# The output layer of the dense block by seven products a quad instead of eight, with sums held in PSUM banks and carried by ScalarE copies

## The chip, the cores and the metric

The kernel runs on one core of a Trainium2 chip (trn2). The metric is the device time of one execution in microseconds, from the median of several runs. The core has TensorE (PE in the profile, with PEld for its weight loads), VectorE (DVE), ScalarE (ACT), GpSimd (POOL) and SyncE (SP), whose queue issues nearly all DMAs.

## What is computed

```python
y = chunked_scan(x, a, B, C)                      # 4 x 8 heads, 768 tokens, 32 wide
x = y as 3072 tokens x 256
p = domain_probs / domain_probs.sum(-1)
out = sum over e < 4 of p[:, e] * (relu(x @ w1[e]) @ w2[e])       # w1: 256 x 1024, w2: 1024 x 256
g, val = out @ w_gate, out @ w_val                                # both 256 x 1536
result = (g / (1 + exp(-g)) * val) @ w_out                        # w_out: 1536 x 256
```

All of it is float32; the dense weights arrive as float64. The last two lines are the dense block. The change is in how its last product, with `w_out`, is formed.

## The kernel before

**Numbers.** A float32 operand is split into a high part (rounded by a ScalarE copy, `high`, or by the activation itself) and a low part (operand minus high part, `low`, one subtraction). A product of a 128x128 weight block with 512 tokens is three matmuls of 512 columns: high·high, low·high, high·low. "Product" below means such three matmuls; `product` (L932 to L936) issues them.

**Stages.** Until about 210 us the scan and the first expert units run. Then `blocks` of experts follow, 32 quads of 45 matmuls, until 552 us. Beside them `dense_quad` turns the float64 dense weights into split float32 blocks and sums of blocks, a step at a time, and stores them in DRAM (`wd_d`, `wo_d`); its steps stand in the table `todo` under slots, four to a quad. From 552.7 us the dense block runs: three pairs of token blocks (2 x 512 tokens each), and in each pair six quads of 256 hidden features, 18 quads.

**A dense quad.** The hidden layer of a quad is two halves, the gate and the value. Each is a 2x2 block product (two feature blocks by two token blocks, 256 inputs in two blocks) done with seven products in Winograd's form instead of eight (`seven`): A11·B11, S2·T2, S1·T1, S3·T3, A12·B21, S4·B22, A22·T4, where S and T are sums and differences of weight blocks and of token blocks made ahead. They go to four PSUM banks X, Y, Z, W (`h0`, `h1`, `h2`, `d0`), and VectorE adds the banks together through the SBUF tiles `c1`, `u` and `v`: `u` = Y + c1 (L957), `v` = Z + u (L959). The gate half adds `v` and `u` to W and Z (L1084) and takes Silu (L1085); the value half does the same adds (L1088) and multiplies with the gate's four results (L1090). Each of the four activations, named 11, 12, 21, 22 by feature block and token block, is split by `parts` (ScalarE L1095, GpSimd L1097).

**The output layer before.** `dense_project` (L1106 to L1131) multiplies each of the four split activations with two 128x128 blocks of `w_out` (two halves of the 256 outputs): eight products a quad, accumulated over the six quads of a pair in four banks (`d1`, `d2`, `o0`, `o1`). It lags a quad: `project_part` puts one activation, two products, at each of four places between the hidden products of the next quad. At the end of a pair the four banks are copied out and stored (`store`).

**What sets the order.** The program is recorded in order (`manual_schedule`) and each engine's queue is served in that order. A PSUM bank, an SBUF cell or a weight buffer is waited for by the instruction that needs it, and everything behind that instruction on its engine waits with it. Weights are loaded by SP two quads ahead (`dense_load`, 16 buffers in `wpool`). `dense_tokens` makes the split tokens and token sums of the next pair on ScalarE and GpSimd, spread over the quads by `dtodo`.

In the expert stage the seven products of a quad are already done with ScalarE copies that carry sums from bank to bank inside PSUM (`expert_hidden`):

```python
add(X, A11, "B11", True)
S.activation(out=Y, in_=X, func=AF.Copy)     # L996, then project_part: six matmuls
add(Y, S2, "T2")                             # accumulates on the copy
S.activation(out=Z, in_=Y, func=AF.Copy)     # L999
```

Of the kernel before, what the change touches and what calls it, by code (L numbers as in the profile page):

```python
# [7 lines left out]
F32 = mybir.dt.float32  # L8
# [16 lines left out]
def kernel(ctx: ExitStack, tc: tile.TileContext, nat_d, bc_d, bc0_d, a_d, probs, w1, w2, wg, wv, wo, out):  # L25
# [74 lines left out]
    wo_d = dram.tile([NQD, P, 2, 2 * DM], F32, name="wo_d")  # L100
# [503 lines left out]

    hid = {}
# [137 lines left out]
    def dense_quad(g, what):  # L743
# [34 lines left out]
        def s2():  # L778
            V.tensor_tensor(out=r["m"], in0=r["m"], in1=r["lo"], op=ALU.add)
            r["m"] = r["m"].bitcast(F32)  # L780
            if what < 2:
                r["s"] = r["f"].rearrange("p k n w -> p (k n w)").bitcast(F32)[:, :2 * FQ]
                gate_sums(r["m"], r["s"])

        def s3():
            if what < 2:
                r["out"] = [dpools["cv"].tile([P, W7], F32R, tag=f"w{z}", name=f"wd_{z}") for z in "hl"]
                high(r["out"][0][:, RAW], r["m"][:, P:])
            else:
                r["out"] = [dpools["cv"].tile([P, 2, 2 * DM], F32R, tag="wo", name="wd_o")]  # L790
                high(r["out"][0][:, 0, :], r["m"])

        def s4():
            if what < 2:
                low(r["out"][1][:, RAW], r["m"][:, P:], r["out"][0][:, RAW])
            else:
                low(r["out"][0][:, 1, :], r["m"], r["out"][0][:, 0, :])
# [7 lines left out]
        def store(z=None):  # L805
            if z is None:
                nc.sync.dma_start(out=wo_d[g], in_=r["out"][0].bitcast(F32))
            else:
                nc.sync.dma_start(out=wd_d[g, what, :, z, :], in_=r["out"][z].bitcast(F32))
# [6 lines left out]
    def dense_load(p, q):  # L816

        for what in range(3):
            if (p, q, what) in wq:
                continue  # L820
            if what < 2:
                hi, lo = (wpool.tile([P, W7], F32R, tag="w", name=f"wq_{z}") for z in "hl")
                for z, v in enumerate((hi, lo)):
                    nc.sync.dma_start(out=v.bitcast(F32), in_=wd_d[q, what, :, z, :])
            else:
                both = wpool.tile([P, 2, 2 * DM], F32R, tag="w", name="wq_o")
                nc.sync.dma_start(out=both.bitcast(F32), in_=wo_d[q])
                hi, lo = both[:, 0, :], both[:, 1, :]
            wq[p, q, what] = hi, lo


# [106 lines left out]
    def temp(tag):  # L938
        if tag == "c1":
            return mpool.tile([P, BN], F32, tag="mb", name=tag)  # L940
        return dpools["dt" if tag == "s" else "uv"].tile([P, BN], F32, tag=tag, name=tag, bufs=5 if tag == "s" else 1)

    pending = []

    def seven(p, w, out):

        X, Y, Z, W = (bank(*b) for b in (banks[0], banks[1], banks[2], banks[3]))
        V = nc.vector
        put = lambda ps, a, v, start: product(ps, w, a, operand(p, v), start)
        c1, u, v = temp("c1"), temp("u"), temp("v")  # L950
        put(X, A11, "B11", True)
        nc.scalar.activation(out=c1, in_=X, func=AF.Copy)
        for fn in pending:
            fn()
# [8 lines left out]
        def rest():  # L963
# [3 lines left out]
            if later[0]:  # L967
                later[0]()
# [435 lines left out]
```

## Time and profile before

| What | us |
|---|---|
| median of 3 runs (833.66 to 834.08) | 833.82 |
| span of the profiled execution, first to last instruction | 832.4 |
| a quad of experts without a wait, 45 matmuls | 10.20 |
| a dense quad, 66 matmuls | 14.96 |

For the profiled execution the page gives the span alone; the median of the timed runs is 1.42 us above it, and no other time of that execution is given. In the profile a matmul of 512 columns has a span of 0.39 us, but such matmuls are pipelined and start every 0.227 us, so spans must not be added up; distances between starts are what counts. ScalarE's spans overlap in the same way. DVE and POOL spans follow each other.

### The profile page before, as it was taken

How to read it: one execution, taken by the hardware profiler on the slowest of the kernel's cores; microseconds unless marked ns; L12 is line 12 of the kernel's file. 1: busy time of each engine (PE TensorE's matmuls, PEld its weight loads, DVE VectorE, ACT ScalarE, POOL GpSimd, SP SyncE). 2: the span in 40 equal slices, each digit the busy share in tenths (PEclk: the TensorE clock that was granted, in tenths of full speed). 3: DMA queues.
4: the chain of work that ended last, by engine and by line, in shares of the span. 5: the costliest groups of instructions: out<-in, count | busy, mean ns of one | idle time of the engine just before them, and what ended most of it. 6: DMA issues, size and time to landing. Idle time of an engine off the chain costs nothing.

```text
span 832.4 us, 12687 instructions
## 1 busy us (share of the span) xinstructions
PE 822.5 (99%) x4417; PEld 683.7 (82%) x4417; DVE 539.0 (65%) x830; ACT 488.4 (59%) x977; POOL 444.6 (53%) x448
## 2 busy tenths in 40 slices
PE   8999999999999999999999999999999999999997
PEld 7998888888778888888888888888888888888886
DVE  6777668565245946665657576648667676676675
ACT  6888777666465566667766666654444444444343
POOL 2665775434397424687785355406756358444351
PEclk9999999999999999999999999999999999999999
DMA  7875546551210153544323231763544365427301
GB/s 245 273 238 160 165 153 196 190 173 50 89 39 30 41 196 120 171 143 132 118 96 121 95 120 48 251 262 133 179 158 159 123 224 184 157 96 257 109 1 52
DMA packets 53296, 119.61 MB, mean 144 GB/s; under 512 B 5424, under 2 KB 19824, under 8 KB 53232
## 3 DMA queue, kind: packets, MB, share of 16 engines
q1 hardware_dynamic: 53088, 118.67, 42.3%
q8 instruction: 35, 0.57, 0.3%
q14 instruction: 29, 0.24, 0.1%
q10 hardware_dynamic: 144, 0.13, 0.0%
HBM read 101.34 MB, written 17.45 MB: 143 GB/s over the span
## 4 chain that ended last, share of the span: by engine, by line
PE 95%; ACT 2%; DVE 1%; issue 1%; ACTq 0%; DVEq 0%
PE h L936 30%; PE h L616 10%; PE d L1042 10%; PE po L1042 10%; PE po L624 10%; PE d L936 8%; PE po L1125 6%; PE d L1125 6%; PE scores L468 1%; PE ypsum L539 1%; PE ypsum L484 1%; DVE acc L679 0%; ACT we_h L687 0%; PE ypsum L497 0%; PE direct L221 0%
## 5 line engine op out<-in xcount | busy, mean ns | idle before, releaser
L1097 POOL TENSOR_TENSOR al<-s,ah 128x512 fp32r<-128x512 f32 x70 | 102.6, 1489 | 144.1 <-ACT ah L1095 112.2
L1095 ACT ACTIVATE ah<-s 128x512 fp32r<-128x512 f32 x72 | 45.3, 632 | 83.4 <-DVE s L1090 83.4
L1007 DVE TENSOR_TENSOR d<-d,c 128x512 f32<-128x512 f32 x32 | 22.4, 699 | 101.5 <-ACT c L1004 101.5
L658 DVE SCALAR_TENSOR_TENSOR hl<-h,hh 128x512 fp32r<-128x512 f32 (+1 forms) x80 | 46.3, 583 | 59.7 <-ACT hh L657 59.4
L991 DVE SCALAR_TENSOR_TENSOR hl<-h,hh 128x512 fp32r<-128x512 f32 x96 | 66.1, 689 | 20.6 <-PE d L1042 15.8
L1042 PE MATMUL po<-hh,we_o 128*128 128x512 f32 x256 | 78.9, 389 | 0.5 <-DVE acc L679 0.5
L1042 PE MATMUL d<-hh,we_o 128*128 128x512 f32 x256 | 78.8, 389 | 0.0
L990 ACT ACTIVATE hh<-h 128x512 fp32r<-128x512 f32 x96 | 57.1, 597 | 27.7 <-DVE h L1011 23.3
L657 ACT ACTIVATE hh<-h 128x512 fp32r<-128x512 f32 (+1 forms) x80 | 40.2, 509 | 52.8 <-PE h L616 52.4
L1085 ACT ACTIVATE s<-s 128x512 f32<-128x512 f32 x54 | 34.0, 632 | 45.5 <-DVE s L1084 44.7
L426 ACT ACTIVATE L<-L,cum 128x128 f32<-128x128 f32 x176 | 56.0, 394 | 4.8 <-POOL L L419 4.8
L616 PE MATMUL h<-xh,w_h 128*128 128x512 f32 (+1 forms) x160 | 56.7, 354 | 1.3 <-DVE hl L658 0.8
L624 PE MATMUL po<-hh,w_h 128*128 128x512 f32 (+1 forms) x160 | 56.4, 353 | 0.6 <-DVE tmp L677 0.6
L1042 PEld LDWEIGHTS po<-hh,we_o 128*128 128x128 f32 x256 | 48.0, 188 | 10.8 <-ACT we_o L687 0.9
L1042 PEld LDWEIGHTS d<-hh,we_o 128*128 128x128 f32 x256 | 48.1, 188 | 10.0
L936 PE MATMUL h<-xh,wq_h 128*128 128x512 f32 x144 | 56.1, 390 | 0.0
L936 PE MATMUL h<-xh,wq_l 128*128 128x512 f32 x144 | 56.0, 389 | 0.0
L936 PE MATMUL h<-xl,wq_h 128*128 128x512 f32 x144 | 56.0, 389 | 0.0
L616 PE MATMUL h<-xl,w_h 128*128 128x512 f32 (+1 forms) x160 | 55.6, 348 | 0.0
L624 PE MATMUL po<-hl,w_h 128*128 128x512 f32 (+1 forms) x160 | 55.5, 347 | 0.0
L616 PE MATMUL h<-xh,w_l 128*128 128x512 f32 (+1 forms) x160 | 55.5, 347 | 0.0
L624 PE MATMUL po<-hh,w_l 128*128 128x512 f32 (+1 forms) x160 | 55.4, 346 | 0.0
(244 smaller groups left out, 2385.0 us busy)
## 6 DMA issues: line engine op xcount, KB each, us to landing
wq_h<-wd_d SPq DMA_DIRECT2D x36, 448.0 KB
wq_l<-wd_d SPq DMA_DIRECT2D x36, 448.0 KB
L<-crow_d SPq DMA_DIRECT2D x22, 512.0 KB
bc<-in_bc_dram SPq DMA_DIRECT2D x21, 512.0 KB
wq_o<-wo_d SPq DMA_DIRECT2D x18, 512.0 KB
raw_q<-in_w_dram SPq DMA_DIRECT2D x32, 256.0 KB
pbc<-probs_d SPq DMA_DIRECT2D x22, 256.0 KB
wd_d<-wd_h SPq DMA_DIRECT2D x12, 448.0 KB
```

Source lines behind the costliest of these rows:

```text
L426: nc.scalar.activation(out=L[:, h, :], in_=L[:, h, :], func=AF.Exp, bias=cols(cum, q)[:, h:h + 1])
L616: nc.tensor.matmul(ps, w[:, k, fs], v[:, k, :], start=(i == 0), stop=(i == len(ops) - 1))
L624: nc.tensor.matmul(po[d], w[:, fc, dsl], x, start=(first and i == 0), stop=(last and i == 2))
L657: nc.scalar.activation(out=hh, in_=ph, func=AF.Relu)
L658: nc.vector.scalar_tensor_tensor(out=hl, in0=ph, scalar=0.0, in1=hh.bitcast(F32), op0=ALU.max, op1=ALU.subtract)
L936: nc.tensor.matmul(ps, x[:, ws], y, start=(start and i == 0), stop=(i == 2), skip_group_check=True)
L990: S.activation(out=hh, in_=ps, func=AF.Relu)
L991: return lambda: V.scalar_tensor_tensor(out=hl, in0=ps, scalar=0.0, in1=hh.bitcast(F32), op0=ALU.max, op1=ALU.subtract)
L1042: nc.tensor.matmul(po[d], both[:, z, dsl], y, start=(first and i == 0), stop=(last and i == 2), skip_group_check=True)
L1095: nc.scalar.activation(out=ah, in_=av, func=AF.Copy)
L1097: low.tensor_tensor(out=al, in0=av, in1=ah.bitcast(F32), op=ALU.subtract)
L1125: nc.tensor.matmul(po[d][:, z:z + n], x[:, dsl], y[:, z:z + n], start=(first and i == 0), stop=(last and i == 2), skip_group_check=True)
```

## The change

**Weights.** `w_out` now goes through the same seven-block preparation as the other two dense weights: sums by `gate_sums` on GpSimd, two more high parts and low parts, and six stores instead of one. Plain blocks go to `wp_d`, the three sums to `ws_d`. The steps of all 18 weight quads start at the slots in `starts`, and the load stands two slots ahead of its first use instead of three.

**Hidden layer.** `seven` is replaced by `dense_gate` and `dense_value`. The sums go from bank to bank by ScalarE copies (`scopy`), as in the expert stage, and by VectorE adds that write back to a bank (`vadd`).

**Output layer.** A quad has seven products: three "side" products with the sums T1, T2, T3 of activations and the weight sums (`side_product`), which accumulate over a pair in banks `d1`, `o0`, `o1`, and four "plain" ones (`plain_product`), which all go through bank `d2`, one kind for all six quads and then the next kind. VectorE makes the sums: two in `dense_value`, and `second_sum` and `fourth_sum` in the next quad's gate half. Activations therefore stay in SBUF for a long time, in cells handed out by `grab` from the list `free`, split parts in cells of the list `rounded`; `drop` puts a cell back at the end of the list. At the end of a pair VectorE combines the banks (`chores`). `hooks` puts the products at the places that `project_part` had. In the first pair a place holds one product or none, later two at most places, and 20 plain products are left for the end of the program. `feed` splits a plain activation ahead of its use; from the second pair on one low part a quad is made on VectorE (`flush`), the others on GpSimd.

```diff
-        late = [(s5, 0, CALM), (lambda: store(0), 1, ANY), (s6, 0, ANY), (lambda: store(1), 1, ANY)]
-        return [(load, 0, ANY), (s0, 3, EARLY), (s1, 2, SUMS), (s2, 1, SUMS), (s3, 2, CALM), (s4, 1, ANY)] + (
-            late if what < 2 else [(store, 3, ANY)]
-        )
+        return [
+            (load, 1, ANY), (s0, 2, EARLY), (s1, 2, SUMS), (s2, 1, SUMS), (s3, 2, CALM), (s4, 1, ANY),
+            (s5, 0, CALM), (lambda: store(0), 1, ANY), (s6, 0, ANY), (lambda: store(1), 1, ANY),
+        ]
...
-    def seven(p, w, out):
...
+    def split(v, engine):
+        h, l = grab(rounded), grab(rounded)
+        nc.scalar.activation(out=h, in_=v, func=AF.Copy)
+
+        def rest(engine):
+            low(l, v, h, engine)
+            drop(v)
...
+    def dense_start(i, what, hook):
...
+        put(X, A11, "B11", True)
+        nc.scalar.activation(out=Y, in_=X, func=AF.Copy)
+        for fn in behind:
+            fn()
+        behind.clear()
+        hook(0)
...
+    def dense_gate(i, hook):
+
+        put, X, Y, Z, W, s = dense_start(i, 0, hook)
+        put(Y, S2, "T2")
+        scopy(Z, Y)
+        hook(1)
+        put(W, S3, "T3", True)
+        c, v = grab(), grab()
+        scopy(c, W)
+        put(Z, S1, "T1")
+        scopy(v, Z)
+        for key in KEYS:
+            s[key] = early.pop(0) if early and key % 10 == 1 else grab()
+        vadd(s[22], W, v)
+        hook(2)
+        put(X, A12, "B21")
+        scopy(s[11], X, AF.Silu)
+        scopy(s[22], s[22], AF.Silu)
+        put(Y, A22, "T4")
+        vadd(s[21], Y, c)
+        put(Z, S4, "B22")
+        scopy(s[12], Z, AF.Silu)
+        drop(c, v)
+        behind.append(lambda: scopy(s[21], s[21], AF.Silu))
+        hook(3)
+
+    def dense_value(i, hook):
+
+        put, X, Y, Z, W, s = dense_start(i, 1, hook)
+        put(Z, S1, "T1", True)
+        put(Y, S2, "T2")
+        u, v = grab(), grab()
+        scopy(u, Y)
+        hook(1)
+        vadd(v, Z, u)
+        put(W, S3, "T3", True)
+        vadd(Y, W, v)
+        hook(2)
+        put(X, A12, "B21")
+        for key, ps in ((11, X), (22, Y)) if i < NQD else ((22, Y), (11, X)):
+            vadd(s[key], ps, s[key], ALU.mult)
+        put(Z, S4, "B22")
+        vadd(Z, Z, u)
+        put(W, A22, "T4")
+        t = tsum[i] = [grab() for _ in range(3)]
+        h12 = s[12] if i < NQD else Z
+        vadd(h12, Z, s[12], ALU.mult)
...
+        if i < NQD:
+            last()
+        vadd(t[T1], h12, s[11], ALU.subtract)
+        vadd(t[T3], s[22], h12, ALU.subtract)
+        if i >= NQD:
+            last()
+        drop(u, v)
+        hook(3)
...
+    def second_sum(i, engine=nc.vector):
+        a, t = acts[i], tsum[i]
+        engine.tensor_tensor(out=t[T2], in0=a[22], in1=t[T1], op=ALU.subtract)
+
+    def fourth_sum(i, engine=nc.vector):
+        a, t = acts[i], tsum[i]
+        engine.tensor_tensor(out=a[12], in0=a[21], in1=t[T2], op=ALU.subtract)
...
-            for what in range(3):
-                at = a
-                for fn, gap, parts in dense_quad(g, what):
...
-                a += 7 if what < 2 else 5
+        starts = [2, 6, 14, 22, 26, 34, 38, 46, 54, 58, 66, 70, 78, 86, 90, 98, 102, 110]
+        for z, start in enumerate(starts):
+            at = n0 + start
...
+            def fill_b():
+                if i == 0:
+                    before(parts[2 * what])
+                elif what == 0:
+                    if i > NQD or i == 1:
+                        plain()
+                    if i > 1:
+                        side_product(i - 2, T3)
+                elif i > 1:
+                    plain()
...
+            def gate(h):
+                if h == 0:
+                    flush()
+                    if i > 0:
+                        if i > NQD:
+                            side_split(i - 1, T1)
+                        feed(1, i, ahead)
+                    hidden_load(i + 1, 0)
+                    fill_b()
+                elif h == 1:
+                    fill_a()
+                    if 0 < i <= NQD:
+                        side_split(i - 1, T1)
+                elif h == 3:
+                    if i > 0:
+                        second_sum(i - 1)
+                    chore(3)
+                    if i > 0:
+                        fourth_sum(i - 1)
+                    token_steps()
...
+            def value(h):
+                if h == 0:
+                    fill_b()
+                elif h == 1:
+                    hidden_load(i + 1, 1)
+                    if full:
+                        feed(1, i, ahead, None if i < len(quads) - 1 else nc.gpsimd)
+                    if i > 0:
+                        side_split(i - 1, T3)
+                        side_split(i - 1, T2)
...
+                    if i >= NQD - 1:
+                        feed(1 if turn else 4 if late_pair else 2, i, ahead)
+                    token_steps()
+                elif h == 2:
+                    fill_a()
```

Three places show how the order changes. The first is on PE, at the start of a gate half in the first pair (the fourth quad): the bank `h0` is X, `h1` is Y, `d0` is W, `h2` is Z; `o1` and `o0` are the side banks, `d1` and `d2` before are the output banks. Before:

```order
L936 MATMUL h0_6732<-xh0_78,wq_h_6396 128x512
L936 MATMUL h0_6732<-xh0_78,wq_l_6397 128x512
L936 MATMUL h0_6732<-xl0_82,wq_h_6396 128x512
L936 MATMUL h1_6733<-t24h_0_92,wq_h_6396 128x512
L936 MATMUL h1_6733<-t24h_0_92,wq_l_6397 128x512
L936 MATMUL h1_6733<-t24l_0_93,wq_h_6396 128x512
L936 MATMUL h2_6734<-xh1_79,wq_h_6396 128x512
L936 MATMUL h2_6734<-xh1_79,wq_l_6397 128x512
L936 MATMUL h2_6734<-xl1_83,wq_h_6396 128x512
```

The same place now:

```order
L945 MATMUL h0_6539<-xh0_78,wq_h_6440 128x512
L945 MATMUL h0_6539<-xh0_78,wq_l_6441 128x512
L945 MATMUL h0_6539<-xl0_82,wq_h_6440 128x512
L972 MATMUL o1_6444<-ds_6323,wq_s_6375 128x512 x2
L972 MATMUL o1_6444<-ds_6324,wq_s_6375 128x512
L945 MATMUL h1_6540<-t24h_0_92,wq_h_6440 128x512
L945 MATMUL h1_6540<-t24h_0_92,wq_l_6441 128x512
L945 MATMUL h1_6540<-t24l_0_93,wq_h_6440 128x512
L972 MATMUL o0_6452<-dr0_6176,wq_s_6375 128x512 x2
L972 MATMUL o0_6452<-dr1_6177,wq_s_6375 128x512
L945 MATMUL d0_6542<-t3h_0_94,wq_h_6440 128x512
```

Before, X, Y and Z are three banks of their own and nothing stands between them; now Y is summed on top of X's copy, with one side product of three matmuls between X's last matmul and Y's first.

The second place is VectorE in the value half of a quad in the second pair (names as above, `s`, `ds`, `xl0`, `acc3` and the like are SBUF cells). Before:

```order
L957 TENSOR_TENSOR u_7415<-h1_7411,c1_7414 128x512 [waits DVE_49,PE_49,Activation_49]
L959 TENSOR_TENSOR v_7416<-h2_7412,u_7415 128x512 [waits DVE_49,PE_49]
L1088 TENSOR_TENSOR v_7416<-d0_7413,v_7416 128x512 [waits DVE_49,PE_49]
L1090 TENSOR_TENSOR s_7376<-v_7416,s_7376 128x512 [waits DVE_49]
L1090 TENSOR_TENSOR s_7388<-h0_7410,s_7388 128x512 [waits PE_49]
L1088 TENSOR_TENSOR v_7416<-h2_7412,u_7415 128x512 [waits DVE_49,PE_49]
L1090 TENSOR_TENSOR s_7393<-v_7416,s_7393 128x512 [waits DVE_49]
L1088 TENSOR_TENSOR u_7415<-d0_7413,u_7415 128x512 [waits PE_49]
L1090 TENSOR_TENSOR s_7399<-u_7415,s_7399 128x512 [waits DVE_49]
```

The same place now:

```order
L1116 TENSOR_TENSOR ds_6186<-h2_7207,ds_6199 128x512 [waits Activation_49,Pool_49]
L1116 TENSOR_TENSOR h1_7206<-d0_7208,ds_6186 128x512 [waits DVE_49,PE_49]
L1116 TENSOR_TENSOR xl0_6879<-h1_7206,xl0_6879 128x512 [waits DVE_49]
L1116 TENSOR_TENSOR ds_6185<-h0_7205,ds_6185 128x512 [waits PE_49]
L1116 TENSOR_TENSOR h2_7207<-h2_7207,ds_6199 128x512 [waits PE_49]
L1116 TENSOR_TENSOR h2_7207<-h2_7207,xl0_6879 128x512 [waits DVE_49]
L1116 TENSOR_TENSOR acc3_89<-h2_7207,ds_6185 128x512 [waits DMAHW7_49,DVE_49]
L1116 TENSOR_TENSOR ds_6196<-xl0_6879,h2_7207 128x512
L1116 TENSOR_TENSOR d0_7208<-d0_7208,ds_6199 128x512 [waits PE_49]
L1116 TENSOR_TENSOR xl1_6881<-d0_7208,xl1_6881 128x512 [waits DVE_49]
L692 TENSOR_TENSOR ds_6320<-ds_6197,ds_6319 128x512 [waits Activation_49]
```

Nine instructions become ten, and a low part follows them; the sums T1 and T3 stand before the last two, which release the bank W (`d0`).

The third place is ScalarE in the fourteenth expert quad, from the copy of X into Y to the copy of W (`we` and `wd` are parts of expert and dense weights, `dr` and `f` their raw forms). Before:

```order
L996 ACTIVATE h_4281<-h_4280 128x512
L687 ACTIVATE we_h<-raw_q 128x512
L687 ACTIVATE we_o<-raw_q 128x512
L687 ACTIVATE we_h<-raw_q 128x384
L687 ACTIVATE wd_h<-f_4050 128x512
L767 ACTIVATE dr<-f_4217 128x512
L768 ACTIVATE f_4217<-f_4217 128x512
L999 ACTIVATE h_4282<-h_4281 128x512
L1001 ACTIVATE c_4284<-d_4283 128x512
```

The same place now:

```order
L1019 ACTIVATE h_4313<-h_4312 128x512
L689 ACTIVATE we_h<-raw_q 128x512
L689 ACTIVATE we_o<-raw_q 128x512
L689 ACTIVATE we_h<-raw_q 128x384
L1022 ACTIVATE h_4314<-h_4313 128x512
L1024 ACTIVATE c_4316<-d_4315 128x512
```

Six weight steps between the copy into Y and the copy into Z have become three.

## Rows read from the trace of the kernel before

**Rows 1.** The page's head, and busy time, share and instructions by engine.

```profile
span 832.4 us, 12687 instructions
...
PE 822.5 (99%) x4417; PEld 683.7 (82%) x4417; DVE 539.0 (65%) x830; ACT 488.4 (59%) x977; POOL 444.6 (53%) x448
```

**Rows 2.** The page's chain that ended last, shares by engine.

```profile
PE 95%; ACT 2%; DVE 1%; issue 1%; ACTq 0%; DVEq 0%
```

**Rows 3.** Expert stage: length, busy PE, PEld, DVE, ACT, POOL, granted clock, DMA.

```profile
239.70:547.40 307.70, 307.18 (x1352) 253.10 (x1351) 194.89 (x292) 198.26 (x357) 181.66 (x204) 1.00 0.36 122
```

**Rows 4.** The chain in order of time: start, length (us), what.

```profile
239.73 2.04 PE h L936 x9
...
547.43 2.04 PE h L936 x9
552.87 2.04 PE h L936 x9
...
597.75 2.04 PE h L936 x9
```

**Rows 5.** Instructions at 362 us: start, length, engine, line, idle before.

```profile
361.88 0.58 ACT L999 ACTIVATE h<-h 128x512 f32<-128x512 f32 x1
361.95 0.39 PE L1042 MATMUL d<-hl,we_o 128*128 128x512 f32 x1
...
362.51 0.50 PE L936 MATMUL h<-xh,we_h 128*128 128x512 f32 x1 [0.17 <-ACT h L999]
362.85 0.40 PE L936 MATMUL h<-xh,we_l 128*128 128x512 f32 x1
```

**Rows 6.** Instructions at 301 to 303 us: from a matmul to ScalarE to VectorE.

```profile
301.43 0.39 PE L936 MATMUL h<-xl,we_h 128*128 128x512 f32 x1
...
301.86 0.60 ACT L1004 ACTIVATE c<-h 128x512 f32<-128x512 f32 x1 [1.38 <-PE h L936]
...
302.49 0.70 DVE L1007 TENSOR_TENSOR d<-d,c 128x512 f32<-128x512 f32 x1 [5.28 <-ACT c L1004]
```

**Rows 7.** VectorE pairs at 303 us (independent) and 623 us (second needs first).

```profile
303.17 0.69 DVE L991 SCALAR_TENSOR_TENSOR hl<-h,hh 128x512 fp32r<-128x512 f32 x1
...
303.78 0.69 DVE L1011 TENSOR_TENSOR h<-h,c 128x512 f32<-128x512 f32 x1
...
623.45 0.69 DVE L1088 TENSOR_TENSOR v<-d,v 128x512 f32<-128x512 f32 x1
...
624.17 0.69 DVE L1090 TENSOR_TENSOR s<-v,s 128x512 f32<-128x512 f32 x1
```

**Rows 8.** Lines L1090 and L1097: shortest, median and longest (ns).

```profile
L1090 DVE TENSOR_TENSOR s<-v,s x36: 691/752/1269, 564.1 to 821.2; 128x512 f32<-128x512 f32 x36
L1090 DVE TENSOR_TENSOR s<-u,s x18: 691/1069/1075, 569.3 to 824.4; 128x512 f32<-128x512 f32 x18
...
L1097 POOL TENSOR_TENSOR al<-s,ah x70: 1280/1302/1759, 565.6 to 821.5; 128x512 fp32r<-128x512 f32 x70
```

**Rows 9.** POOL's groups for two pairs' tokens, 560 to 832 us: busy, mean ns, idle.

```profile
L690 POOL TENSOR_TENSOR xl<-acc,xh 128x512 fp32r<-128x512 f32 x8 | 11.3, 1409 | 0.0
...
L690 POOL TENSOR_TENSOR t24l<-acc,t24h 128x1024 fp32r<-128x1024 f32 x2 | 4.8, 2402 | 0.0
```

**Rows 10.** ScalarE at the first Silu of the dense block, 556 to 558 us.

```profile
556.77 1.28 ACT L1085 ACT_TABLE_LOAD   x1 [2.52 <-DVE s L1084]
558.07 0.63 ACT L1085 ACTIVATE s<-s 128x512 f32<-128x512 f32 x1
```

**Rows 11.** The end, 827 to 829 us.

```profile
827.67 0.28 PE L1125 MATMUL po<-al,wq_o 128*128 128x256 f32 x1
...
828.40 0.42 DVE L1139 COPY ob<-po 128x256 f32<-128x256 f32 x1 [0.37 <-ACT ob L1141]
```

**Rows 12.** A raw dense weight's load, issued on SP.

```profile
489.36 0.38 SPq L758 DMA_DIRECT2D f<-in_wg_dram  x1
```

**Rows 13.** The ScalarE step that waited for that load.

```profile
493.72 0.66 ACT L767 ACTIVATE dr<-f 128x512 f32<-128x512 f32 x1 [0.50 <-DMA f<-in_wg_dram]
```

More of the change, by code (lines that the diff above doesn't have):

```diff
@@ L602, in points @@
         }
+    quads = [(p, q) for p in range(NPAIR) for q in range(NQD)]
     hid = {}
@@ new lines, with vadd @@
+    behind = []
+    def dense_start(i, what, hook):
+        p, q = quads[i]
+        w = wq.pop((i, what))
+        X, Y, Z, W = (bank(*b) for b in banks[:4])
+        put = lambda ps, a, v, start=False: product(ps, w, a, operand(p, v), start)
+        put(X, A11, "B11", True)
[4 more added lines that the diff above has]
+        hook(0)
+        return put, X, Y, Z, W, acts.setdefault(i, {})
+    def vadd(out, x, y, op=ALU.add):
+        nc.vector.tensor_tensor(out=out, in0=x, in1=y, op=op)
@@ new lines, with chore, loads_ahead, feed @@
+    order = [(p, k) for p in range(NPAIR) for k in range(4 * NQD)]
+    to_split = list(order)
+    to_load = [(p, k) for p, k in order if k % 3 == 0]
+    def chore(n=1):
+        for _ in range(n):
+            if chores:
+                chores.pop(0)()
+    def loads_ahead(n):
+        while to_load and to_load[0] in order[:n]:
+            p, k = to_load.pop(0)
+            plain_load(p, k // 3)
+    def feed(n, done, ahead=5, engine=nc.gpsimd):
+        for _ in range(n):
+            if ahead > 24 and len(rounded) < 8:
+                return
+            for pk in to_split:
+                if pk not in order[:ahead]:
+                    return
+                if pk[0] * NQD + pk[1] % NQD < done:
+                    to_split.remove(pk)
+                    plain_split(*pk, engine)
+                    break
@@ L1146, with plain @@
+    def plain(n=1):
+        for _ in range(n):
+            plain_product(*order.pop(0))
     with tc.manual_schedule():
@@ L1329 @@
[L1329 to L1337 removed]
+            for j, fn in enumerate(dense_tokens(p + 1, True)):
+                at = ((1, 1, 3, 4, 4, 5, 6, 6, 7, 7, 9, 10), (17, 17, 17, 17, 17, 18, 18, 19, 20, 21, 21, 22))[p][j]
+                dtodo.setdefault(at, []).append(fn)
@@ new lines, in hooks, with fill_a @@
+        def hooks(i, what):
+            p, q = quads[i]
+            full = i >= NQD
+            turn = q == NQD - 1 and p < NPAIR - 1
+            late_pair = i > 2 * NQD
+            ahead = 40 if late_pair else 8 if i >= NQD - 3 else 5
+            def fill_b():
[8 more added lines that the diff above has]
+                    plain()
+            def fill_a():
+                for fn in late:
@@ L1347 @@
+        plain()
+        side_product(n - 2, T3)
+        plain()
+        side_product(n - 2, T2)
+        steps = [None, None, None, T1, None, T3, None, T2]
+        while order:
+            feed(1, n, 24, nc.vector)
+            k = steps.pop(0) if steps else None
+            if k is not None:
+                side_product(n - 1, k)
+            chore()
+            plain()
         assert not todo, list(todo)
```

382 lines of the change are left out of this document (231 added, 151 removed).

## The prediction

> **What bounds the kernel.** I read the page's head first, then the chain of waits, the expert stage as one stretch, the chain in order of time, and last single instructions and lines. The reader is to see a kernel whose time is nearly the number of its matmuls. PE is busy 822.5 of 832.4 us and the next engine, VectorE, 65% [rows 1]. The chain that ended last is 95% PE [rows 2]. The expert stretch of 307.70 us has 307.18 of PE, with all of the full clock granted, the 2.4 GHz level [rows 3]. Each line of the chain in time is the first nine matmuls of a half: from 552.87 to 597.75 are three dense quads, so a quad of 66 matmuls takes 44.88 / 3 = 14.96 us and a matmul 0.2267 us [rows 4]. A product of three is then 0.68 us. Forty-five matmuls are 10.20 us, so thirty expert quads should take 306.0; they take 547.43 − 239.73 = 307.70 [rows 4]. The other 1.70 us are short waits.
>
> The profiled execution lasted 832.4 us by its span [rows 1]; the page gives no other time. The median of the runs is 833.82, 1.42 above it. I work out differences in the span and subtract them from the median.
>
> **What is removed.** Eight products a quad become seven, over 18 quads: 18 products, 54 matmuls, times 0.2267 = **−12.24 us**. All are on the path, since PE has no idle time to absorb them. Everything below asks how much of that waits give back.
>
> **Lags.** From a matmul's start to a ScalarE copy of its bank: 301.86 − 301.43 = 0.43; the copy takes 0.60; VectorE follows 0.03 later [rows 6]. From a copy's end to the waiting matmul: 361.88 + 0.58 = 362.46 to 362.51, 0.05. The matmul after one that waited starts 0.34 later, not 0.23, so a wait costs another 0.11 [rows 5]. VectorE takes one step per 0.61 us when they are independent and per 0.72 when each needs the last [rows 7].
>
> **Expert stage.** More ScalarE and GpSimd steps prepare `w_out`, but the table `starts` spaces all steps anew. Before, up to six weight steps stood between the copy into Y and the copy into Z, and the wait at 362.51 ends with that second copy [rows 5]. Now the runs are shorter. At best all 1.70 us come back, at worst none; I take **−1.2**, as the long runs are gone but four steps in a row remain. The load has a slot less of lead; that is a rival below.
>
> **The dense quads.** Counted in matmuls, the second quad is now 48 or 10.88 us, the third to sixth 54 or 12.24, the seventh 60 or 13.60, the others 63 or 14.28, and the last has the left-over products behind it.
>
> Quad 1. No output product exists yet. The first Silu of the block needs a table load of 1.28 us [rows 10]. Before, it began after ScalarE had been idle 2.52 us and was hidden beneath VectorE; now it stands directly behind the copy `v`. From Z's last matmul: copy to 1.03, load to 2.31, Silu of X to 2.91, PE at 2.96. The value half's first product wants X ten matmuls later, at 2.27. That is 0.69 + 0.11 = **+0.8**. It is zero if ScalarE gets there earlier, 1.4 if one more Silu, 0.63 [rows 10], stands in the way. In the trace the first Silu starts 0.02 after the load's end (558.05 to 558.07) [rows 10]. The Trainium skill's page "ScalarE: Activation LUTs", section "What ACT_TABLE_LOAD costs", adds a drain of about 1.38 us to the load; the idle time ahead of it could have hidden that here, and by the page this term would be 2.2, an estimate.
>
> Quad 2. The first plain product stands straight behind X and needs a low part made just before it; the bank W waits for VectorE and Z for a Silu. Each is a chain of the lags above that ends 0.35 to 0.5 us late: **+1.4**, between 0 and 2.8 (twice the lateness).
>
> Quads 3 to 7. In the gate half one product stands between X's last matmul and Y's first, which sums on the copy. The copy is ready at 0.43 + 0.60 + 0.05 = 1.08; PE is there after four pitches, 0.907. So 0.17 + 0.11 = 0.28, five times: **+1.4**. If the copy took 0.58 and started at once this would be 1.2; behind one Silu on ScalarE (0.63 [rows 10]) it would be 4.5. In the value half Z's product stands there as well, and nothing waits. From the eighth quad two or more products fill the gate's place.
>
> Quads 8 to 18. The tightest hand-over is bank W of the value half. From Y's last matmul: copy `u` done at 1.03, then ten VectorE steps at most 0.72 apart, 8.3 us, or 7.9 with the independent pairs. W is wanted 37 matmuls later, at 8.39. The slack of 0.1 to 0.5 holds on average, not each time: **+1.1**, a tenth of a us in each of eleven quads, between 0 and 2.2. VectorE's total, twelve steps of 0.72 from PSUM and three wholly in SBUF at 0.75 to 1.07 [rows 8], is 10.9 to 11.8 of 14.28: it keeps up. The ends of the first two pairs add three VectorE steps each: **+0.4**, between 0 and 1.5.
>
> The end. Between the last matmul's end, 827.67 + 0.28 = 827.95, and the last copy's, 828.40 + 0.42 = 828.82, lie 0.87 us, for two copies in turn [rows 11]. Now one half's addition runs beneath the other half's matmuls, and one of 0.42 remains: **−0.45**, between 0 and −0.5. The products at the end need low parts, ten of them on VectorE, which has little else then.
>
> Sum: −12.24 − 1.2 + 0.8 + 1.4 + 1.4 + 1.1 + 0.4 − 0.45 = −8.79. 833.82 − 8.79 = **825.0 us**.
>
> **Rivals.**
>
> *VectorE is held up by GpSimd, and the time ends slower.* The place is quads 3 to 6: four sums there (T1, T2, T3 and the fourth) have both inputs in SBUF, beside ten steps from PSUM, and GpSimd makes low parts all the while. Steps of this kind took 0.69 to 1.27 us, GpSimd's 1.28 to 1.76 [rows 8]: they lengthen one another. At 1.27 a quad needs 10 × 0.72 + 4 × 1.27 = 12.28 us of 12.24, no loss. If each waited out a whole GpSimd step, 0.69 + 1.29 = 1.98, it needs 15.1: +2.9 × 4, +1.5 in the seventh, and 12 × 0.72 + 3 × 1.98 = 14.6 against 14.28 in eleven later ones, +3.3; together +16.3, **841.3**. It decides from a mean of 1.27 on and makes the kernel slower from about 1.7. Halfway, at 1.6, it gives 832. Against it: no step was longer than 1.27. The Trainium skill's page "SBUF — State Buffer", section "Who interferes with whom", calls the port that the two share an exclusive lock whose loser is fully blocked, a VectorE instruction with two SBUF inputs among them; the rows show both stretched rather than one blocked for all of the other's 1.28 us.
>
> *The expert stage gives it back.* A raw load landed 493.72 − 489.36 = 4.36 us after its issue, and ScalarE waited 0.50 us for it [rows 12, 13]. Now each has two slots, 5.1 us, instead of 7.65. Whatever waits for it on ScalarE has the copy into Z queued behind. If all 18 loads cost 0.50, and none of the 1.2 is won: 826.2 + 9.0 = **835.2**; if half do, 830.7. For it: a load was late even with three slots. Against: a load that lands as that one did has 0.7 us to spare.
>
> *GpSimd falls behind.* In quads 9 to 12 it makes six low parts a quad and the next pair's token parts: four of 1.41, one of 2.40 [rows 9], five more at 1.28, 14.4 us over three quads, 4.8 each. At 1.30 a low part this is 12.6 of 14.28. With every step at the longest, 1.76 instead of 1.30, it is 17.1: +2.8 over three and a half quads, +9.9, **834.9**. Cells come back late, and ScalarE's copies wait for them. Against: the median is 1.30 [rows 8], and low parts are made ahead.
>
> *Nothing is won.* The products go but as many waits appear everywhere: about 833.8. Nothing in the rows speaks for it.
>
> **How the numbers follow.** Forecast 0.71, VectorE 0.11, loads 0.08, GpSimd 0.08, nothing won 0.02. The forecast's own range takes the bounds of the terms, not all at once: 820.5 to 829.5. The rivals' milder forms lie up to 832, so the range is 820.5 to 832.0, with about 0.12 left out above it and 0.04 below. A difference under 0.2%, 1.67 us, can't be told from none here: faster is below 832.15, slower above 835.49. Faster: 0.71 + 0.06 + 0.05 + 0.02 = 0.84. Slower: 0.04 + 0.01 + 0.04 + 0.01 = 0.10. Within: 0.06. Each is summed over the forecast and the rivals in that order; the forecast lies wholly in faster.
>
> **What the profile will show.** If right: 54 fewer matmuls, PE's share still about 98%; 30 expert quads in about 306.5 us; in quads 3 to 7 a PE wait of some 0.17 us for ScalarE's copy at each gate's Y; quads 8 to 17 at 14.3 to 14.5 us; one wait of 0.7 us for a Silu behind the table load; one VectorE addition behind the last matmul. It is wrong if PE's waits in the dense block end with VectorE for half a us or more in each quad, if expert quads are over 10.3, or if ScalarE in quads 9 to 12 waits for GpSimd.

## The result and the profile after

The changed kernel takes 825.14 us (median of 4 runs, 824.71 to 825.44); the kernel before, beside it, 833.74. The ratio is 0.9899, 95% interval 0.9885 to 0.9913: faster by 1.0%. The forecast was 825.0. Its parts came out less evenly than its total, which is what the experiments are about.

The page of the changed kernel, its span and busy times, and the shares of the chain that ended last:

```profile
span 823.0 us, 12879 instructions
PE 812.4 (99%) x4363; PEld 671.6 (82%) x4363; DVE 562.4 (68%) x862; ACT 551.7 (67%) x1108; POOL 499.7 (61%) x513
...
PE 93%; ACT 2%; POOL 2%; DMA 1%; issue 1%; DVE 1%; DVEq 0%; POOLq 0%; ACTq 0%
```

Against [rows 1, 2]: 4417 − 4363 = 54 matmuls fewer, the span 9.4 us shorter, and PE as full as before. ScalarE has 63 us more and GpSimd 55, and still PE sets the time.

To see where the 9.4 us lie I cut the span at two PE instructions that both kernels have: one at the last expert work in front of the blocks, ended by the same VectorE step, and the first matmul of the dense block. First the kernel before, then the changed one:

```profile
234.89 0.70 PE L1042 MATMUL po<-hh,we_o 128*128 128x512 f32 x2 [0.50 <-DVE acc L679]
...
552.71 0.39 PE L936 MATMUL h<-xh,wq_h 128*128 128x512 f32 x1
```

```profile
234.09 0.70 PE L1065 MATMUL po<-hh,we_o 128*128 128x512 f32 x2 [0.49 <-DVE acc L681]
...
551.17 0.39 PE L945 MATMUL h<-xh,wq_h 128*128 128x512 f32 x1
```

And the end of the changed kernel, which answers to [rows 11]:

```profile
818.13 0.87 PE L972 MATMUL d<-t24l,wq_o 128*128 128x256 f32 x6
818.33 0.69 DVE L1268 TENSOR_TENSOR xh<-h,xh 128x512 f32<-128x512 f32 x1 [1.27 <-PE h L972]
819.04 0.76 DVE L1268 TENSOR_TENSOR acc<-d,acc 128x256 f32<-128x256 f32 x2
```

| stretch | before | after | difference |
|---|---|---|---|
| up to the first mark | 234.89 | 234.09 | −0.80 |
| to the dense block, experts | 317.82 | 317.08 | −0.74 |
| dense block, to the last matmul's end (827.95, 819.00) | 275.24 | 267.83 | −7.41 |
| rest | 4.45 | 4.00 | −0.45 |
| span | 832.4 | 823.0 | −9.40 |

The dense block is 12.24 − 7.41 = 4.83 us longer than its missing matmuls alone would make it. These are waits, and four kinds of them make up 4.5 us. (A wait is counted here as the distance between two matmul starts beyond 0.2267, the 0.1 after it included.)

Quad 1, ScalarE and PE:

```profile
556.81 0.60 ACT L1119 ACTIVATE ds<-h 128x512 f32<-128x512 f32 x1
557.42 1.28 ACT L1119 ACT_TABLE_LOAD   x1
558.72 0.60 ACT L1119 ACTIVATE xh<-h 128x512 f32<-128x512 f32 x1
...
559.37 0.50 PE L945 MATMUL h<-xh,wq_h 128*128 128x512 f32 x1 [0.56 <-ACT xh L1119]
...
559.71 0.40 PE L945 MATMUL h<-xh,wq_l 128*128 128x512 f32 x1
```

The copy `v`, the table load and the Silu follow one another without a gap, and the first value product waits for the Silu's end: 0.72 + 0.11 = 0.83.

Quad 2, the first plain product, which waits for GpSimd's low part (0.65 with what follows; two further waits of the quad are 0.25 and 0.28, 1.18 in all):

```profile
567.35 1.28 POOL L692 TENSOR_TENSOR dr<-xh,dr 128x512 fp32r<-128x512 f32 x1 [2.96 <-issue]
...
568.69 0.50 PE L972 MATMUL d<-dr,wq_o 128*128 128x512 f32 x1 [0.37 <-POOL dr L692]
```

Quads 3 to 7, here the first of five: one side product between X's copy and Y's first matmul, which starts 0.38 after the last and not 0.23. With the 0.11 after it, five times, 1.32:

```profile
580.09 0.58 ACT L1108 ACTIVATE h<-h 128x512 f32<-128x512 f32 x1 [1.92 <-PE h L945]
...
580.35 0.39 PE L972 MATMUL o<-ds,wq_s 128*128 128x512 f32 x1
...
580.73 0.50 PE L945 MATMUL h<-t24h,wq_h 128*128 128x512 f32 x1
581.06 0.39 PE L945 MATMUL h<-t24h,wq_l 128*128 128x512 f32 x1
```

From quad 8 on there are only four waits, about 1.1 together: two where VectorE also ends a sum of output blocks (L1268; 0.30 and 0.25), one for bank W (0.20), and one where ScalarE's copy of `d2` stood behind seven roundings (0.39). The first of them, VectorE and PE: X is multiplied only at the end of the row marked x2, and PE waits for it.

```profile
699.03 0.68 DVE L1268 TENSOR_TENSOR xh<-d,xh 128x512 f32<-128x512 f32 x1
...
699.63 1.28 DVE L1116 TENSOR_TENSOR ds<-h,ds 128x512 f32<-128x512 f32 x2
...
700.96 0.50 PE L945 MATMUL h<-xh,wq_h 128*128 128x512 f32 x1
```

### The profile page after: what moved, and what is told of

Same layout as the page of the kernel before. It is cut to its first block, busy times and chain, and to the rows that moved or that the text cites. A ratio compares the mean times of both kernels' runs of the same rounds, so it can differ in the third digit from the quotient of the medians.

```text
span 823.0 us, 12879 instructions
## 1 busy us (share of the span) xinstructions
PE 812.4 (99%) x4363; PEld 671.6 (82%) x4363; DVE 562.4 (68%) x862; ACT 551.7 (67%) x1108; POOL 499.7 (61%) x513
## 4 chain that ended last, share of the span: by engine, by line
PE 93%; ACT 2%; POOL 2%; DMA 1%; issue 1%; DVE 1%; DVEq 0%; POOLq 0%; ACTq 0%
PE h L945 31%; PE d L1065 10%; PE po L1065 10%; PE h L618 10%; PE po L626 10%; PE d L945 7%; PE d L972 6%; PE o L972 3%; PE ypsum L540 1%; PE scores L469 1%; PE h L972 1%; DMA L<-crow_d 1%; PE ypsum L485 1%; POOL acc L849 1%; POOL xl L692 0%
## 5 line engine op out<-in xcount | busy, mean ns | idle before, releaser
L945 PE MATMUL h<-xh,we_h 128*128 128x512 f32 x128 | 50.0, 391 | 0.4 <-ACT c L1027 0.4
L1065 PE MATMUL po<-hl,we_o 128*128 128x512 f32 x128 | 49.8, 389 | 0.0
L945 PE MATMUL h<-xl,we_h 128*128 128x512 f32 x128 | 49.8, 389 | 0.0
```

What stands on the lines that cost most here:

```text
L945: nc.tensor.matmul(ps, x[:, ws], y, start=(start and i == 0), stop=(i == 2), skip_group_check=True)
L1065: nc.tensor.matmul(po[d], both[:, z, dsl], y, start=(first and i == 0), stop=(last and i == 2), skip_group_check=True)
```

## The experiments

**An eighth product put back.** The T3 side product is done twice.

```diff
-        products(accs[p, k], wq[i, 2][2 - k], sides[i, k], q == 0, q == NQD - 1)
+        products(accs[p, k], wq[i, 2][2 - k], sides[i, k], q == 0, q == NQD - 1 and k != T3)
+        if k == T3:
+            products(accs[p, k], wq[i, 2][2 - k], sides[i, k], False, q == NQD - 1)
```

> The T3 side product is done twice in every quad (so that sum counts twice): 18 products of three matmuls more, all else as in the changed kernel. Theory, that the gain is the 54 matmuls and the waits are what they cost: +12.24 us, less the 1.3 us of waits between X and Y in quads 3 to 7, which the second product fills: about 836.1 us, slower than the kernel before by some 2.3. Rival, that the time has come from the new order and the ScalarE copies and not from the matmuls: 826 to 830 us, as the waits swallow the extra products.

835.5 us, ratio to before 1.0021 (1.0012 to 1.0030); the dense block takes 278.21. That is 10.38 more than 267.83, or 12.24 − 1.86, near the theory's 12.24 − 1.3, and no wait at Y is left. The gate of the third quad there, PE:

```profile
581.05 0.39 PE L972 MATMUL o<-ds,wq_s 128*128 128x512 f32 x1
581.27 0.39 PE L945 MATMUL h<-t24h,wq_h 128*128 128x512 f32 x1
```

With as many matmuls as before, the new form is 278.21 − 275.24 = 2.97 us slower in the dense block. The whole gain in the dense block is the matmuls that are not there.

**Four matmuls between X and Y.** In quads 3 to 7 only, the first of the T2 product's three matmuls, `(0,)`, goes in front of Y:

```diff
...
                         side_product(i - 2, T3)
+                        if i <= NQD:
+                            side_product(i - 2, T2, (0,))
...
-                        side_product(i - 2, T2)
+                        side_product(i - 2, T2, (1, 2) if i <= NQD else range(3))
```

> In quads 3 to 7 the first matmul of the T2 side product is moved up in front of Y, so that four matmuls and not three stand between X and Y; nothing is added. Theory, that PE waits there for ScalarE's copy alone: the copy is ready 1.08 us after X's last matmul starts, PE now comes at 5 x 0.2267 = 1.13, so five waits of 0.26 go: 823.8 us and no wait of that kind in the trace. Rival, that VectorE, late from its lengthened sums, is what these quads really run at: the time stays at 825.1 and the waits show up at another place of the same quads.

824.47 us; ratio to before 0.9889 (0.9876 to 0.9903). The five waits for the copy are gone, yet the dense block takes 267.64, only 0.19 less. The rival is right in that the waits come up elsewhere in the same quads: W now waits for VectorE's last step of the half before, as here in quad 6 (VectorE and PE):

```profile
618.80 0.69 DVE L1118 TENSOR_TENSOR t24h<-d,t24h 128x512 f32<-128x512 f32 x1
...
619.17 0.39 PE L974 MATMUL o<-ds,wq_s 128*128 128x512 f32 x1
...
619.55 0.50 PE L945 MATMUL d<-t3h,wq_h 128*128 128x512 f32 x1
```

VectorE ends at 619.49 and PE goes on 0.06 later. The wait at Y had hidden this one behind it.

**The table load earlier.** A Silu of eight columns goes behind the first copy of X into Y.

```diff
+        if i == 0 and what == 0:
+            scopy(dpool.tile([P, 8], F32, name="warm", tag="warm"), X[:, :8], AF.Silu)
```

> A Silu of 8 columns is put behind the first copy of the dense block on ScalarE, where ScalarE is idle, so that the table load stands there. Theory, that the wait of 0.83 us at the first value half is the load: it goes, 824.3 us. If a drain stood beside the load (the Trainium skill, page ScalarE: Activation LUTs, section What ACT_TABLE_LOAD costs), the row would show some 1.4 us between the load and its neighbours, an estimate of that page. Rival, that three Silus in a row are late there anyway: 0.3 to 0.6 us of the wait stay, 824.6 to 824.9.

824.8 us (0.9889, 0.9876 to 0.9903); the dense block takes 267.07, 0.76 less, and PE has no wait in quad 1. ScalarE there:

```profile
553.42 0.58 ACT L1108 ACTIVATE h<-h 128x512 f32<-128x512 f32 x1 [1.38 <-PE h L945]
554.02 1.28 ACT L1121 ACT_TABLE_LOAD   x1
555.31 0.18 ACT L1121 ACTIVATE warm<-h 128x8 f32<-128x8 f32 x1
```

The load costs its 1.28 us and nothing beside it: the copy ends at 554.00, the Silu starts 0.01 after the load. The changed kernel shows the same (557.41, 557.42, 558.70, 558.72). The drain that the Trainium skill's page "ScalarE: Activation LUTs", section "What ACT_TABLE_LOAD costs", adds to it is not seen here.

**The even starts.** Only the table is put back.

```diff
-        starts = [2, 6, 14, 22, 26, 34, 38, 46, 54, 58, 66, 70, 78, 86, 90, 98, 102, 110]
+        starts = [4, 11, 18, 23, 30, 37, 42, 49, 56, 61, 68, 75, 80, 87, 94, 99, 106, 113]
```

> Only the table of starts is put back to the even spacing of the kernel before (4, 11, 18, 23, 30, ...), with the seven-block steps of w_out kept. Theory, that the uneven table is what took the waits out of the expert quads: three to six waits of 0.44 us come back, +1.3 to +2.6, 826.4 to 827.7 us. Rival, that the dense steps of w_out being spread into more and shorter pieces did it, whatever the table: 825.1 within 0.3.

848.69 us; ratio to before 1.0176 (1.0163 to 1.0190), slower than the kernel before. From the first mark to the dense block it takes 575.22 − 234.77 = 340.45 us, 23.4 more. Neither theory had this size. Two places cost 8 us each; ScalarE and PE at the first:

```profile
304.31 0.52 ACT L689 ACTIVATE wd_h<-dr 128x384 fp32r<-128x384 f32 x1 [8.99 <-DMA wd_d<-wd_h]
...
305.21 0.59 ACT L1019 ACTIVATE h<-h 128x512 f32<-128x512 f32 x1
...
305.86 0.80 PE L945 MATMUL h<-t24h,we_h 128*128 128x512 f32 x1 [7.59 <-ACT h L1019]
```

ScalarE stands before writing the high part of the next weight until the store of the last one has read its buffer, and the copy of X into Y is queued behind. Stretches of the same kernel (length, then busy PE, PEld, DVE, ACT, POOL; granted clock; DMA share and GB/s):

```profile
298.00:305.80 7.80, 0.26 (x2) 0.00 (x0) 0.45 (x1) 1.49 (x4) 0.34 (x1) 0.83 0.75 248
305.80:310.00 4.20, 4.14 (x10) 3.27 (x11) 0.24 (x1) 2.87 (x6) 1.91 (x2) 0.50 0.69 217
310.00:315.00 5.00, 5.00 (x24) 4.11 (x23) 2.79 (x5) 2.48 (x5) 0.00 (x0) 1.00 0.96 293
```

After nearly 8 us without work PE runs for 4 us at a granted clock of 0.50, the 1.2 GHz level, 10 matmuls where there would be 18.

**The same with two buffers.** The even starts stay; the high weight parts get a second buffer.

```diff
-            r["out"] = [dpools["cv"].tile([P, W7], F32R, tag=f"w{z}", name=f"wd_{z}") for z in "hl"]
+            r["out"] = [dpools["cv"].tile([P, W7], F32R, tag=f"w{z}", name=f"wd_{z}", bufs=2 if z == "h" else 1) for z in "hl"]
```

> As the run before it with the even starts (848.7 us), but with two buffers for the high weight parts that ScalarE writes and SP stores. Theory, that ScalarE waited there for a store to give the single buffer back (the idle time of 9 us ends with the store, 6 us after its issue) with the copy into Y queued behind it: both 8 us waits of PE and the stretches at a granted clock of 0.63 behind them go, 848.7 - 16 - 5 = about 828 us. Rival, that the raw loads landed late or that ScalarE has too many steps in a row: the waits stay or shrink by a third, 840 to 849 us.

833.98 us, ratio to before 1.0008 (0.9988 to 1.0028): no difference from the kernel before is shown, and its ten times lie as far apart as 831.96 and 839.67. The two long waits are gone, 14.7 us, so the store's buffer was their cause. But 9.1 us stay between the first mark and the dense block (326.15 against 317.05). Some 6 of them are three waits of PE, 1.95, 2.08 and 1.74 us, each behind a raw load on which ScalarE waited. About 1.6 are the 3.4 us at a granted clock of 0.50 that follow the first of them, eight matmuls 0.43 apart and not 0.23. The rest are shorter waits. What SP waited for ahead of the first of these loads, then GpSimd, SP, ScalarE and PE at 300 us:

```profile
SPq L760 <- POOL wd_l L692: 8.0, 1, 8.0
...
295.06 1.29 POOL L692 TENSOR_TENSOR wd_l<-f,wd_h 128x512 fp32r<-128x512 f32 x1 [0.97 <-ACT wd_h L689]
...
296.38 0.38 SPq L760 DMA_DIRECT2D f<-in_wg_dram  x1
...
300.69 0.66 ACT L769 ACTIVATE dr<-f 128x512 f32<-128x512 f32 x1 [2.97 <-DMA f<-in_wg_dram]
...
301.79 0.58 ACT L1022 ACTIVATE h<-h 128x512 f32<-128x512 f32 x1
...
302.43 0.50 PE L945 MATMUL h<-xh,we_h 128*128 128x512 f32 x1 [1.78 <-ACT h L1022]
```

The load lands 4.31 us after its issue, two steps and the copy follow, and PE loses 2 us. This is the load rival by its effect, but the shorter lead alone does not explain it: a load sent at its slot would have 5.1 us. The raw loads have two buffers (`raw_p`), and a weight quad's sums are written into its raw tile (`r["s"]`), so the tile is held until GpSimd has made the low part of the sums. That step ends at 296.35, and the load goes out 0.03 later; SP had issued nothing since the load before it, at 269.26, and the last 8.0 us of its wait end there. The loads at 414.09 and 467.83, behind the other two waits, go out 0.03 after such a step as well. With seven blocks `w_out` holds its raw tile this long too. Such low parts held the loads up for 42.5 us in all here and for 3.2 in the changed kernel. In the kernel before it was 47.5, but there the step stood a slot later behind the load, and ScalarE waited for landings only 1.6 us in all. No run was made with a third raw buffer or a third slot, so what each of the two is worth is not shown. The expected 828 was too low because I had counted one cause. (The 0.63 named ahead of this run is a mean over a granted clock of 0.50 and then 1.00.)

**Three edits together.** The early load, four matmuls between X and Y, and VectorE's order (`last()` releases W). Of the edit only the last part is shown:

```diff
...
-        vadd(h12, Z, s[12], ALU.mult)
+        if i >= NQD:
+            vadd(h12, Z, s[12], ALU.mult)
...
         if i < NQD:
             last()
+            vadd(h12, Z, s[12], ALU.mult)
...
-        for key, ps in ((11, X), (22, Y)) if i < NQD else ((22, Y), (11, X)):
+        for key, ps in ((11, X), (22, Y)):
```

> Three edits to the changed kernel together: the early Silu table load, four matmuls between X and Y in quads 3 to 7, and VectorE's order in the value half so that bank W is released before the product of 12 (first pair) and X before Y (later pairs). Theory, that the waits of these places are single hand-overs: -0.83 (table), -1.30 (X to Y) without the four new waits of 0.11 to 0.26 for W that the second edit alone gave, -0.54 (X behind the pair ends): 825.14 - 2.7 = 822.5 us. Rival, that VectorE as a whole is late there: the waits move again, 823.8 to 824.5.

825.58 us (0.9904, 0.9889 to 0.9919), a miss. At the end of quad 7 it is 1.36 us ahead of the changed kernel; then ten waits of 0.2 to 0.3 for W, one of which was there before, give it all back, and the dense block takes 268.39. From the eighth quad on X's product ends late, so taking X first makes VectorE stand still (0.47 us at 655.3 us, in quad 8) and delays its whole chain.

**A sum made twice.**

```diff
         engine.tensor_tensor(out=t[T2], in0=a[22], in1=t[T1], op=ALU.subtract)
+        engine.tensor_tensor(out=t[T2], in0=a[22], in1=t[T1], op=ALU.subtract)
```

> The second sum, one with both inputs in SBUF, is made twice in each quad by VectorE (the same result). Such sums took 0.68 to 2.76 us in the changed kernel. Theory, that they stand in time in which VectorE waits anyway (it was idle 0.75 to 1.46 us before the value half's first step): most is absorbed, some quads lose 0.2 to 0.5, 826 to 828 us. Rival, that VectorE's total bounds these quads: 18 x 1.2 us, 840 us or more.

829.24 us (0.9945, 0.9930 to 0.9960): more than expected, far less than the rival. The dense block takes 271.44, +3.61 for 18 sums, more than half of it in quads 3 to 7. VectorE and PE in quad 4:

```profile
602.90 1.67 DVE L1197 TENSOR_TENSOR acc<-xh,acc 128x512 f32<-128x512 f32 x1
604.49 0.68 DVE L1116 TENSOR_TENSOR ds<-h,ds 128x512 f32<-128x512 f32 x1
...
605.22 0.50 PE L945 MATMUL h<-xh,wq_h 128*128 128x512 f32 x1 [0.44 <-DVE ds L1116]
```

The value half's first step starts straight behind the sums, and PE waits for it. In the first pair VectorE has no room for a further sum.

**All low parts on GpSimd.**

```diff
-                        feed(1, i, ahead, None if i < len(quads) - 1 else nc.gpsimd)
+                        feed(1, i, ahead, nc.gpsimd)
```

> The one low part a quad that VectorE makes from the second pair on goes to GpSimd, seven a quad there. Theory, that GpSimd has room (7 x 1.30 = 9.1 of 14.28 us, 13.9 with token steps) and that the low part on VectorE stands off the path: 825 to 826.5 us. Rival, that GpSimd is at its limit in the second pair: a loss of 1.3 us and more in three or four quads and ScalarE waiting for cells, 829 to 832.

825.22 us (0.9901, 0.9886 to 0.9916); the dense block takes 267.65, 0.18 less, as the wait of 0.20 for W is gone. The low part on VectorE, named in the change, gains nothing, and GpSimd had room.

**The edits that paid.** As before, with X first only in quads 11 and 17 (`if i < NQD or i in (10, 16)`) and the low parts on GpSimd.

> The changed kernel with: the early table load; four matmuls between X and Y in quads 3 to 7; bank W released before the product of 12 in the first pair only; X before Y in the two quads in which VectorE also ends a sum of output blocks (11 and 17) and in no other; all low parts of the second and third pair on GpSimd. Theory, from the single runs: -0.83, -0.53, -0.5 and -0.2 us in the dense block, 267.8 - 2.05 = 265.8 us from its first matmul to the last matmul's end, and about 823.1 us in all. Rival, that each edit only moves a wait to the next hand-over: the dense block stays above 267.0.

823.81 us, ratio to before 0.9880 (0.9863 to 0.9896); the changed kernel in the same session 825.70, ratio 0.9904 (0.9889 to 0.9918). The dense block takes 266.48: 1.35 less, not 2.05. The 0.5 for the two quads did not come. X no longer waits there, but W does, 0.30 us once and 0.21 once, and the wait for W in quad 11, which was gone with all low parts on GpSimd, is there again (0.21). PE at the first of the two:

```profile
703.98 0.84 PE L974 MATMUL d<-ds,wq_o 128*128 128x512 f32 x3
704.85 0.50 PE L945 MATMUL d<-t3h,wq_h 128*128 128x512 f32 x1
```

Its median is the lowest of all here, though its interval overlaps that of the changed kernel.

**The changed kernel again.** Unaltered.

> The changed kernel once more, unaltered, beside the others. Theory, that the time up to the expert quads scatters by itself: the dense block is again 267.8 us within 0.1, while its first matmul falls anywhere from 550.9 to 552.6 us, as in the kernels that are equal up to there; median 825.1 within 0.7. Rival, that the 0.8 us by which the expert stage began earlier than in the kernel before belong to the change: its first matmul falls at 551.2 again, within 0.2.

825.7 us; the dense block 267.80 against 267.83, the experts 317.05 against 317.08. The two marks, PE:

```profile
235.32 0.70 PE L1066 MATMUL po<-hh,we_o 128*128 128x512 f32 x2 [0.50 <-DVE acc L681]
...
552.37 0.39 PE L945 MATMUL h<-xh,wq_h 128*128 128x512 f32 x1
```

The first mark lies 1.23 us later than in the first profile of the same program. In the other kernels it lies between 233.86 and 235.49. So the 0.80 us ahead of the first mark are scatter, and only the stretches behind it can be compared to a tenth.

**The load one slot ahead.**

```diff
-            (load, 1, ANY), (s0, 2, EARLY),
+            (load, 2, ANY), (s0, 1, EARLY),
```

> The raw load of each dense weight stands one slot (2.55 us) ahead of its first step and not two; starts and all else as in the changed kernel. Theory, that ScalarE's first step waits for the landing, 4.3 us after the issue, and the copy into Z waits behind it: up to 1.7 us in most of 18 places, 840 to 850 us. Rival, that the loads are issued early enough anyway, or that the step stands where ScalarE has nothing urgent behind it: 825 to 828 us.

826.19 us (0.9909, 0.9894 to 0.9924), the time that the rival gave. But the edit moved the loads little: SP takes its queue in order, and they stand behind stores and expert weights there. Counted from the first mark, ten of the eighteen go out within 0.35 us of their time in the changed kernel, and the largest shift is 1.44 us, where a slot is 2.55. So a shorter lead was hardly put to the test. ScalarE waits for landings in both kernels, up to 2.4 us here and 1.9 there, but what is queued behind has time. ScalarE at the one place where PE lost something (0.4 us):

```profile
385.46 0.67 ACT L769 ACTIVATE dr<-f 128x512 f32<-128x512 f32 x1 [2.44 <-DMA f<-in_wg_dram]
386.03 0.66 ACT L770 ACTIVATE f<-f 128x512 int32<-128x512 uint8 x1
386.58 0.59 ACT L1027 ACTIVATE c<-h 128x512 f32<-128x512 f32 x1
```

Here the steps stand behind the copy into Z, and the copy `c` follows. At the even starts they stood ahead of a copy on which PE's next product sums. The wait of 2.44 us cost PE 0.4 here; one of 2.17 cost it 2.1 at 420 us of the kernel with two buffers. Where in the quad a late step stands decides more than how late it is.

## Why the prediction was right, point by point

- **Removed, −12.24.** Right: 54 matmuls fewer, and 54 put back cost 10.38 with the waits that they fill.
- **Quad 1, +0.8.** Right, 0.83, and 0.76 comes back when the load is moved. The rows had the price; no drain came on top.
- **Quad 2, +1.4.** Right, 1.18, in three waits: for the low part, for W and for Z.
- **Quads 3 to 7, +1.4.** Right as a wait (1.32), wrong as a cost: taking it away gains 0.19, since VectorE's release of bank W is up to 0.27 us behind it. With W released earlier (three edits together) these quads are 0.47 shorter. The prediction counted each wait as if nothing stood behind it.
- **Quads 8 to 18, +1.1, and the pair ends, +0.4.** Together 1.1 against 1.5, but not divided as said: W cost 0.20 once, not a tenth in each of eleven quads. The rest was at two places where VectorE ends a sum, and one where a ScalarE copy stood behind seven roundings, which I had not named.
- **Experts, −1.2.** 0.74. The three waits behind six steps in a row, 0.44 each, are gone as the term had it. But the first steps of the new table stand in front of a copy `c` at 242 us, where PE now waits 0.63, and I had not counted that. This term was the one least understood. The table `starts` did not improve the expert stage a little: with the steps of `w_out` added, the old table costs 23.4 us more. I had priced only what the table could win over the kernel before, not what the added steps would cost without it, and had overlooked that the high parts have one buffer, which a store must give back, and the raw loads two.
- **End, −0.45.** Right in size, by luck. I said that one half's addition would run beneath the other half's matmuls. Both start behind the last matmul's end at 819.00, as VectorE was on a whole-width addition until 819.02, and they end 0.79 after it, against 0.87 before. The rest of the gain lies behind the last addition, where the stores land: 3.2 us to the end of the span against 3.6. Why these are shorter is open.
- **The total** is nearer than its parts: the measured sum, −0.74 − 7.41 − 0.45 = −8.6, differs from the forecast −8.79 by little because smaller costs and a smaller gain cancelled. The span's other −0.80 is scatter. In the later session the same two kernels lie 833.62 − 825.70 = 7.92 us apart, so agreement to a tenth is luck.
- **VectorE held up by GpSimd.** I said that no step was longer than 1.27 us and that the rows showed both stretched. The changed kernel shows 36 second and fourth sums from 0.68 to 2.76 us, 12 of them over 1.27. VectorE and GpSimd at 573 us:

```profile
572.94 1.29 POOL L1085 TENSOR_TENSOR acc<-acc,pbc 128x512 f32<-128x512 f32 x1
...
573.60 1.18 DVE L1192 TENSOR_TENSOR acc<-ds,acc 128x512 f32<-128x512 f32 x1
...
574.19 1.75 POOL L692 TENSOR_TENSOR dr<-acc,dr 128x512 fp32r<-128x512 f32 x1
...
574.82 1.67 DVE L1196 TENSOR_TENSOR ds<-xh,acc 128x512 f32<-128x512 f32 x1
```

  They take turns: GpSimd's step ends at 574.23, VectorE's 0.55 later at 574.78, GpSimd's next 1.16 later at 575.94, VectorE's 0.55 later at 576.49. That is how the Trainium skill's page "SBUF — State Buffer", section "Who interferes with whom", describes it, one holder at a time; here the trace agrees, and my reading of [rows 8] was wrong. The rival still fell by its price, but narrowly. In quads 3 to 6, where it was to decide, the four sums had a mean of 1.26 us, just below the 1.27 from which it decides. Over all quads the mean of the 36 is 1.09, since half of them meet no step of GpSimd. How little room was left the sum made twice shows, with 2.1 us more in quads 3 to 7. (Halfway, at 1.6, the rival's working gives 16 × 0.34 = 5.4 us more, so 830.4 and not 832.) The L1116 steps with a bank as an input stayed at 0.68 to 0.70; those without one, the first pair's T1 and T3, took up to 1.78.
- **GpSimd falls behind** did not happen, even with a low part more a quad.
- **The expert stage gives it back** did not happen either: landings held ScalarE up five times, 4.6 us together, and none of these waits reached PE. But I had read [rows 12] wrongly. That load, too, was issued late for its buffer and not for its slots: GpSimd's low part in the kernel before ends at 489.34, and the load goes out at 489.36.

```profile
487.60 1.74 POOL L690 TENSOR_TENSOR wd_l<-f,wd_h 128x512 fp32r<-128x512 f32 x1
```

What stays open: why the time up to the first mark scatters by 1.6 us between profiles of the same instructions, and why the granted clock fell to 0.50, the 1.2 GHz level, after a wait of 2 us at 302 us of the kernel with two buffers, but stayed at 1.00 after one as long at 420 us. No run was made for either.

## What to carry to other kernels

Where one engine is full, count its instructions first; then treat each wait as the first of a row, and look what stands a tenth behind it before pricing its removal. When preparation steps are added to a queue that also carries the copies the full engine waits for, their places are part of the change: price the added steps at the old places too. Look also which buffers the queued loads and stores wait for, since a held buffer holds the whole queue behind it.

## What the runs showed of the hardware

- A wait costs PE about 0.1 us beyond itself: at a granted clock of 1.00 the matmul after the one that waited starts 0.33 to 0.34 later, not 0.23, in every kernel here.
- VectorE steps with both inputs in SBUF took up to 2.76 us beside GpSimd, those with a bank as input never over 0.70.
- A table load in the dense block took 1.28 us; it started within 0.02 of the step before it, and the step after it started within 0.02 of its end.
- After nearly 8 us without work PE ran at a granted clock of 0.50 for about 4 us.
